# Attention with a gated feed-forward: other positions for the outer query products, both score tiles first from block 16 on, weight sums later on GpSimd, and the x addition on GpSimd

## The chip, the core and the metric

One Trainium2 chip, and of it one core. A core has five engines that run their own instruction streams and meet at semaphores: TensorE (PE, matrix products; its weight loads are shown apart as PEld), VectorE (DVE), ScalarE (ACT), GpSimd (POOL) and SyncE (SP), which here issues all the DMAs after the start. PE writes its products to PSUM, eight banks of 128 x 512 floats. The metric is the time of one execution in microseconds; lower is better.

## What is computed

x is 2048 x 512 in bf16. There are 32 heads of width 128, with keys and values of 2048 positions from a cache. The result is

```
xn = layernorm(x)
q  = xn @ wq                                  # per head, 2048 x 128
p  = softmax(q @ k_cache.T * 128**-0.5)
s  = concat(p @ v_cache) @ wo                 # 2048 x 512
gate, up = xn @ W_gate, xn @ W_up             # 2048 x 1792
g  = silu((relu(gate) * up) @ W_down)
out = x + s * g
```

## The kernel before

**Blocks and positions.** The attention is cut into 128 blocks: head h by head, and in each head four query tiles Q of 512 rows. A block has 8 positions. At a position PE multiplies two key tiles of 128 with the query tile (the score pair: two products of 128 x 512, line 1467), ACT takes the exponential of both at once (line 1479), and PE multiplies a pair of such exponentials with the values (8 products of 128 x 129, line 1576, called PV below). PV runs three positions behind the scores, so at each step of the main loop (line 1767) PE gets the score pair of position gp = gq + 3 and the PV of position gq. A block and a position named below are those of gq. When a block's last PV is done, DVE normalizes it (reciprocal and Onorm, lines 1496 and 1499); the first PV of the next block waits for that, since both use the same two PSUM banks.

**The ring.** The other six banks make three slots of two banks (`ring_acquire`, line 389). A score pair takes a slot and gives it back when its exponential is done. Other products on PE, called items, take slots from the same ring and give them back when DVE has read the result. Slots are handed out in turn. A slot that is held (`hold=True`) leaves the ring until `ring_release`, which puts it second in line; meanwhile the score pairs alternate between the two that are left.

**The items.** All the projections that the attention needs are put between score pairs and PV by a plan that is written out by hand (`plan`, filled by `at(block, position, item)`, lines 1642 to 1748); `side` does the same for work that gives PE nothing. The projections use Strassen's seven products. Blocks 0 to 15 carry the rest of the gated feed-forward (`emit_gu`, `emit_d`), the query projections of the first heads (`emit_st`) and sums of weights on POOL (`gu_sums`, `emit_sw`). From block 16 on there are two kinds of items:
- `emit_os`, at position 0 of a block: one step of the output projection of the four heads of the last group of 16 blocks, four steps for four blocks. Steps 0, 1 and 2 give PE 8 products of 128 x 256 and DVE two or three additions; step 3 gives PE 4 products. The blocks of step 3 (those that leave 3 when divided by 4) are called early: there PE issues the score pairs of positions 0 and 1 before the item, and none at position 1.
- `emit_unit`: the query projections of the group of heads after next, as seven units of seven products, 42 units in all: in each stretch of 16 blocks seven, starting in blocks that are two apart, from block 21 to block 113 (`unit_at`, line 941). A unit has six steps. Step 0 takes and holds a slot and issues two products, steps 1, 2 and 3 one each into the same banks, and step 3 releases the slot; in the next block step 4 takes and holds a slot again, and step 5 releases it. Between the steps DVE reads the sums out (line 1038), and a step waits for DVE's reading of the step before. POOL prepares the operands of a unit beforehand (`prep_unit`), and after two of the seven units it adds four sums (`add_unit`, line 1104) on which the next unit's DVE work waits.

**Positions of the unit steps** (line 1720): in the first block 2, 3, 5, 6, in an early block 3, 4, 6, 7; in the second block 3, 5, or 5, 7 if the block after it is early. An item at position 7 is issued ahead of the score pair (`ahead_of_S`).

**Order of scores and PV.** At a position with an item, or while a unit holds a slot, or at position 7 ahead of an early block, PE gets both score tiles and then both PV tiles. At every other position the two are interleaved (`split`, line 1818): score tile, PV tile, score tile, PV tile.

**POOL and DVE beside it.** `emit_wx` (line 1293) scales and sums output weights on POOL, once for 16 blocks; `emit_ox` (line 1308) forms four sums of attention outputs on DVE, twice for 16 blocks. In blocks 117 to 127 `emit_base` (line 1439) makes the part of the output that is known by then, s_acc times g plus x, with two DVE operations for each of 16 tiles.

## Time and profile before

| | us |
|---|---|
| median of 3 runs (lowest, highest) | 1259.94 (1259.73, 1260.38) |
| the profiled execution | 1260.08 |
| its span, first to last instruction | 1258.7 |
| of it outside the span | 1.4 |
| granted TensorE clock | 1.00 throughout |

The rows of the profile itself are shown where they are used. How they are read: a row of the timeline has the start, the duration from the first start to the last end of a merged run, the engine (a q behind it marks the sequencer), the line of the kernel, the operation, what is written and read, its shape, and how many instructions were merged; brackets give the idle time of that engine before it and what ended it. A row of the waits has who waited for whom, the total in us, how often, and the longest. A row of the stretches has, for each engine, busy time and number of instructions. PE's products are pipelined: one of 128 x 512 is shown with 0.38 us, but the next one starts 0.22 us later, so the room that a product takes is read from the starts. A weight load runs beside the products, and its wait is no loss as long as it is over when the product before it is. Some product records are missing from the trace (12130 beside 12353 weight loads); there the starts are further apart without any wait.

### The profile page before, as it was taken

The numbers are of one execution on the slowest core, as the hardware profiler recorded it, in microseconds if no ns is written. First come the engines' busy times: TensorE is split into PE (matmuls) and PEld (weight loads), VectorE is DVE, ScalarE is ACT, GpSimd is POOL, SyncE is SP. The second block draws the span as 40 slices with busy tenths as digits, with TensorE's granted clock in tenths as the row PEclk, the third lists the DMA queues.
The fourth block names the chain that finished last, engine by engine and source line by source line (L and its number), as shares of the span: only waits on it lengthen the run. The fifth ranks groups of instructions, "written<-read, shape, count | busy, mean of one in ns | idle before, by whom it ended". The sixth has DMA issues, their size and how long they took to land.

```text
span 1258.7 us, 29145 instructions
## 1 busy us (share of the span) xinstructions
PE 1237.9 (98%) x12130; PEld 860.1 (68%) x12353; DVE 809.6 (64%) x1328; ACT 1031.1 (82%) x1109; POOL 597.0 (47%) x606
## 2 busy tenths in 40 slices
PE   9999999999999999999999999999999999999998
PEld 5466666776677676667766676667676676767775
DVE  7677877665565747564665647564766547674487
ACT  4457877667888898888888898889888898889994
POOL 3473876415634377343855357534835456530002
PEclk9999999999999999999999999999999999999999
DMA  9712331324122332323222232233222222235222
GB/s 272 155 31 43 72 77 23 54 43 117 40 43 47 77 60 47 52 64 68 51 31 41 66 61 52 47 68 68 48 51 50 43 58 47 51 64 144 59 52 76
DMA packets 254914, 82.25 MB, mean 65 GB/s; under 512 B 226368, under 2 KB 254784, under 8 KB 254784
## 3 DMA queue, kind: packets, MB, share of 16 engines
q1 hardware_dynamic: 254112, 79.98, 30.7%
q8 instruction: 98, 1.61, 0.6%
q10 hardware_dynamic: 672, 0.39, 0.1%
q14 instruction: 32, 0.26, 0.1%
HBM read 40.63 MB, written 4.19 MB: 36 GB/s over the span
## 4 chain that ended last, share of the span: by engine, by line
PE 80%; ACT 9%; issue 8%; DVE 2%; POOL 0%; DMA 0%; DVEq 0%; POOLq 0%
PE ps_acc L1576 30%; PE ps_r L1467 27%; ACT PT L1479 9%; PE ps_r L1348 5%; PE ps_r L1033 5%; PE ps_r L1145 3%; PE ps_r L1206 3%; PE ps_r L711 2%; PE ps_r L715 2%; PE ps_r L896 2%; PE ps_acc L814 1%; DVE UVR L1038 1%; DVE QT_sb L1038 1%; POOL g_sb L1631 0%; DVE OX L1322 0%
## 5 line engine op out<-in xcount | busy, mean ns | idle before, releaser
L1479 ACT ACTIVATE PT<-ps_r 128x1024 bf16<-128x1024 f32 x1024 | 979.8, 1032 | 158.4 <-PE ps_r L1467 151.5
L1576 PEld LDWEIGHTS ps_acc<-V_sb,PT 128*128 128x128 bf16 x8192 | 582.7, 98 | 211.0 <-ACT PT L1479 3.4
L1576 PE MATMUL ps_acc<-V_sb,PT 128*128 128x129 bf16 x8192 | 705.3, 220 | 7.2 <-DVE Onorm L1499 0.3
L1467 PE MATMUL ps_r<-QT_sb,KT_sb 128*128 128x512 bf16 x1835 | 619.1, 380 | 5.8 <-DVE QT_sb L1038 0.9
L1038 DVE TENSOR_TENSOR UVR<-UVR,ps_r 128x512 f32<-128x512 f32 (+1 forms) x228 | 165.7, 755 | 134.1 <-PE ps_r L1033 130.2
L1467 PEld LDWEIGHTS ps_r<-QT_sb,KT_sb 128*128 128x128 bf16 x2048 | 173.2, 98 | 19.4 <-DVE QT_sb L1038 7.3
L1366 DVE TENSOR_TENSOR s_acc<-s_acc,ps_r 128x512 f32<-128x512 f32 x264 | 167.6, 683 | 11.4 <-PE ps_r L1348 10.5
L1496 DVE RECIPROCAL rz_sb<-ps_acc 128x4 f32<-128x4 f32 x127 | 22.9, 181 | 133.6 <-PE ps_acc L1576 132.8
L1005 POOL TENSOR_TENSOR TI<-xn_sb 128x512 f16<-128x512 f16 x48 | 57.7, 1202 | 88.4 <-PE ps_r L1033 88.4
L1038 DVE TENSOR_TENSOR QT_sb<-UVR,ps_r 128x512 bf16<-128x512 f32 x72 | 49.1, 687 | 65.2 <-PE ps_r L1033 62.8
L1499 DVE TENSOR_TENSOR Onorm<-ps_acc,rz_sb 128x512 bf16<-128x512 f32 x127 | 87.8, 691 | 4.4
L979 POOL TENSOR_SCALAR Wq_sb<-Wq_sb 128x1024 bf16<-128x1024 bf16 x12 | 33.2, 2768 | 117.5 <-DMA Wq_sb<-in_A_wq_dram 117.5
L1005 POOL TENSOR_TENSOR TI<-xnT 128x512 f16<-128x512 bf16 x36 | 41.6, 1155 | 71.0 <-PE ps_r L1033 70.2
L1631 POOL TENSOR_TENSOR g_sb<-s_acc,WX 128x512 bf16<-128x512 f32 x6 | 6.8, 1154 | 124.2 <-DVE WX L1624 124.2
L1104 POOL TENSOR_TENSOR QT_sb<-UVR,UVR 128x512 bf16<-128x512 f32 x24 | 32.1, 1367 | 62.3 <-DVE UVR L1038 62.3
L1104 POOL TENSOR_TENSOR UVR<-UVR,UVR 128x512 f32<-128x512 f32 x24 | 29.7, 1269 | 61.5 <-DVE UVR L1038 61.5
L1005 POOL TENSOR_TENSOR TI<-xn_sb,TI 128x512 f16<-128x512 f16 x48 | 55.5, 1156 | 0.0
L1033 PE MATMUL ps_r<-TI,SI 128*128 128x512 f16 x126 | 48.2, 382 | 2.2 <-DVE UVR L1038 2.2
L1348 PE MATMUL ps_r<-WX,OX 128*128 128x256 f16 x336 | 45.8, 273 | 0.0
L1005 POOL TENSOR_TENSOR TI<-xnT,TI 128x512 f16<-128x512 bf16 x36 | 41.6, 1156 | 0.0
L1121 POOL TENSOR_SCALAR gB<-gB 128x512 bf16<-128x512 bf16 x14 | 20.8, 1487 | 42.6 <-DVE gB L1151 42.6
L1348 PEld LDWEIGHTS ps_r<-WX,OX 128*128 128x128 f16 x336 | 32.9, 98 | 9.8 <-ACT PT L1479 1.8
(186 smaller groups left out, 1205.0 us busy)
## 6 DMA issues: line engine op xcount, KB each, us to landing
V_sb<-in_A_v_cache_dram SPq DMA_DIRECT2D x32, 512.0 KB, 4.4
Wq_sb<-in_A_wq_dram SPq DMA_DIRECT2D x16, 256.0 KB, 3.1
Wo_sb<-in_A_wo_dram SPq DMA_DIRECT2D x8, 512.0 KB, 4.7
out_dram<-g_sb SPq DMA_DIRECT2D x4, 512.0 KB, 4.7
g_sb<-out_dram SPq DMA_DIRECT2D x4, 512.0 KB, 6.6
xr_sb<-in_A_x_dram SPq DMA_DIRECT2D x16, 128.0 KB, 2.0
OT_store<-Onorm SPq DMA_TRANSPOSE x127, 2.5
Wd_sb<-in_B_W_down_dram SPq DMA_DIRECT2D x1, 1792.0 KB, 14.5
```

Of the source, the lines that this page charges most:

```text
L1005: return sem_ui.sig(pool.tensor_tensor(dst, x, y, o))
L1033: return sem_up.sig(pe.matmul(dst, lhs, rhs, start=start, stop=stop, skip_group_check=True))
L1038: dve.tensor_tensor(dst, x, ps, ALU.add))
L1104: u_tok["add"] = sem_uv.sig(pool.tensor_tensor(dst, UU[:, i, :], RR[:, i, :], ALU.add))
L1145: ins = pe.matmul(ps_r[:, bank, :], L(i), R(i), start=(i == 0), stop=(i == HC - 1))
L1206: ins = pe.matmul(ps_r[:, bank, j * DH:(j + 1) * DH], L(i), R(i), start=(i == 0 and j == 0), stop=(i == HF - 1 and j == 1))
L1348: ins = pe.matmul(ps_r[:, bank, j * DH:(j + 1) * DH], L(i), R(i), start=(i == 0 and j == 0), stop=(i == GH - 1 and j == 1))
L1366: t = dve.tensor_tensor(names[k], names[k], view(bank), op)
L1467: ins = pe.matmul(ps_r[:, 2 * s + tt, :], KT_sb[h % 2][:, t * 128:(t + 1) * 128], QT_sb[qt_slot[(h, Q)]][:], start=True, stop=True)
L1479: act.activation(PT[pb][:], ps_r[:, 2 * s:2 * s + 2, :], ACTF.Exp, scale=scale / WSC)
L1499: dve.tensor_tensor(Onorm[ob][:], o_ap, rz_sb[:].to_broadcast([128, 4, Dh]), ALU.mult))
L1576: ins = pe.matmul(o_ap, PT[pb][:, tt, j * 128:(j + 1) * 128], V_sb[vb][:, t, 0:VW], start=(t == 0 and j % 2 == 0), stop=(t == KT - 1 and j ...
```

## The change

- The steps of every unit move: to positions 1, 3, 5, 6 in the first block, early or not; in the second to 2, 4, or to 3, 6 if the block after it is early. Nothing is left at position 7, so `ahead_of_S` goes.
- Score and PV tiles are interleaved only below block 16 and only where there is no item. From block 16 on PE always gets both score tiles first.
- `emit_wx` of the groups in the middle is issued two blocks later (position 6 of the tenth block of 16 rather than the eighth).
- `emit_base`: the multiplication stays on DVE, the addition of x goes to POOL, with a semaphore of its own.
- At the start: the scaling of weights on ACT stays where it was, as `gu_scale`; the sums of it on POOL, `gu_sums(0)`, `(1)` and `(2)`, move from the last feed-forward stage and from block 0 to (block, position) (0, 7), (1, 3) and (1, 5), the first behind a wait for the newest exponential, and `emit_sw(1)`, the weights of the second head pair, from ahead of the loop to (1, 1). One copy of a query product from PSUM goes from ACT to DVE.

```diff
@@ gu_sums
+        def gu_scale(k):
+            W = W2[k % NW]
+            _wait(act, gu_tok[(k, "w")])
+            wflat = W[:].rearrange("p c i e -> p (c i e)")
+            gu_tok[(k, "s")] = sem_w2s.sig(act.activation(wflat, wflat, ACTF.Copy, scale=GSC))
+
         def gu_sums(k):
             W, X = W2[k % NW], SG[k % NW]
-            _wait(act, gu_tok[(k, "w")])
-            wflat = W[:].rearrange("p c i e -> p (c i e)")
-            t = gu_tok[(k, "s")] = sem_w2s.sig(act.activation(wflat, wflat, ACTF.Copy, scale=GSC))
-            _wait(pool, t)
+            if (k, "s") not in gu_tok:
+                gu_scale(k)
+            _wait(pool, gu_tok[(k, "s")])
@@ emit_gate_up
                     if fc in (7, 9):
-                        gu_sums((fc - 7) // 2)
+                        gu_scale((fc - 7) // 2)
@@ emit_st, step 0
-                if pr == 0 and c == 1:
-                    _wait_all(act, [p1, st_tok["r"]])
-                    st_tok["u"] = sem_qpa.sig(act.copy(cu[:], ps_r[:, banks[0], :]))
-                else:
-                    _wait(dve, p1)
-                    st_tok["u"] = sem_qpe.sig(dve.tensor_copy(cu[:], ps_r[:, banks[0], :]))
+                _wait(dve, p1)
+                st_tok["u"] = sem_qpe.sig(dve.tensor_copy(cu[:], ps_r[:, banks[0], :]))
@@ emit_base
-            _wait(dve, t1)
-            _wait(dve, sem_xr[k % 4].cur())
-            base_done[n] = sem_fin.sig(
-                dve.tensor_tensor(s_acc[:, n, :], s_acc[:, n, :], xr_sb[:, k % 4, :], ALU.add))
+            _wait(pool, sem_xr[k % 4].cur())
+            _wait(pool, t1)
+            base_done[n] = sem_fb.sig(
+                pool.tensor_tensor(s_acc[:, n, :], s_acc[:, n, :], xr_sb[:, k % 4, :], ALU.add))
@@ the plan of the units
-            first = (3, 4, 6, 7) if b in early else (2, 3, 5, 6)
-            second = (5, 7) if b + 2 in early else (3, 5)
-            for step, (r, p) in enumerate([(0, p) for p in first] + [(1, p) for p in second]):
+            second = (3, 6) if b + 2 in early else (2, 4)
+            for step, (r, p) in enumerate([(0, p) for p in (1, 3, 5, 6)] + [(1, p) for p in second]):
                 at(b + r, p, (emit_unit, 0, n, step))
-            if first[3] == NP - 1:
-                ahead_of_S.add(b)
@@ the main loop
-        emit_sw(1)
...
-            if pq == NP - 1 and bq in ahead_of_S:
-                for it in items:
-                    emit_M(it)
-                items = None
+            split = not ahead and not items and bq < GB
             if not ahead:
                 open_S_pair(gp)
                 emit_S_tile(gp, 0)
+                if not split:
+                    emit_S_tile(gp, 1)
...
+            if (bq, pq) == (0, 7):
+                _wait(pool, sem_exp.cur())
+                gu_sums(0)
+            if (bq, pq) == (1, 1):
+                emit_sw(1)
+            if (bq, pq) == (1, 3):
+                gu_sums(1)
             if pq == 4 and bq == 0:
+                gu_scale(2)
+            if (bq, pq) == (1, 5):
                 gu_sums(2)
...
-            if pq == 6 and bq % GB == 7 and 1 < bq // GB < NG - 1:
+            if (bq % GB, pq) == (9, 6) and 1 < bq // GB < NG - 1:
                 emit_wx(bq // GB)
             if items:
-                if not ahead:
-                    emit_S_tile(gp, 1)
...
-            split = not items and not ahead
-            if split and (u_held or (pq == NP - 1 and bq + 1 in early)):
-                emit_S_tile(gp, 1)
-                split = False
             emit_PV_tile(gq, 0)
             if split:
                 emit_S_tile(gp, 1)
```

More of the change, by code (lines that the diff above doesn't have):

```diff
@@ L270, in bass_recurrent_scan__mha_block_cached__glu_gated_reglu__prompt_kernel @@
         sem_da = newsem()
-        sem_qpa = newsem()
         sem_rz = newsem()
@@ L275, in bass_recurrent_scan__mha_block_cached__glu_gated_reglu__prompt_kernel @@
         sem_fin = newsem()
+        sem_fb = newsem()
         sem_sq = newsem()
@@ L943, in bass_recurrent_scan__mha_block_cached__glu_gated_reglu__prompt_kernel @@
         u_prep = {}
-        ahead_of_S = set()
         u_done = {}
```

## The prediction

> **What bounds the kernel now.** I read the page first, then busy time by stretch, then the waits of PE's weight loads, then timelines of single blocks.
>
> ```profile
> PE 1237.9 (98%) x12130; PEld 860.1 (68%) x12353; DVE 809.6 (64%) x1328; ACT 1031.1 (82%) x1109; POOL 597.0 (47%) x606
> PE 80%; ACT 9%; issue 8%; DVE 2%; POOL 0%; DMA 0%; DVEq 0%; POOLq 0%
> 322.44:1148.39 825.95, 814.40 (x8406) 579.24 (x8559) 507.08 (x814) 726.57 (x761) 418.49 (x428) 1.00 0.28 54
> 1164.30:1172.25 7.95, 7.84 (x89) 5.95 (x89) 5.30 (x10) 7.43 (x9) 0.00 (x0) 1.00 0.19 49
> 1172.25:1180.20 7.95, 7.90 (x89) 5.95 (x89) 5.21 (x10) 7.43 (x9) 0.00 (x0) 1.00 0.51 85
> ```
>
> PE is the bound at a granted clock of 1.00. The change removes no product, so only PE's waits can go, and their size is the first number to find. PE's busy share hides them, because a product is shown longer than its room. The third row is the stretch from the first PV of block 21 to that of block 116, 95 blocks with all 42 units. The last two rows are blocks 118 and 119: no unit, one output step of 8 products, 7.95 us each.
>
> ```profile
> 599.13 0.59 PE L1467 MATMUL ps_r<-QT_sb,KT_sb 128*128 128x512 bf16 x2
> 599.56 1.04 PE L1348 MATMUL ps_r<-WX,OX 128*128 128x256 f16 x8
> 600.43 1.06 PE L1576 MATMUL ps_acc<-V_sb,PT 128*128 128x129 bf16 x12
> 601.33 0.38 PE L1467 MATMUL ps_r<-QT_sb,KT_sb 128*128 128x512 bf16 x1
> 602.20 0.38 PE L1033 MATMUL ps_r<-xnT,Wq_sb 128*128 128x512 bf16 x1
> 602.64 0.62 PE L1576 MATMUL ps_acc<-V_sb,PT 128*128 128x129 bf16 x8
> ```
>
> From the starts: a score pair takes 0.43, an output step of 8 products 0.87, two unit products 0.44 (602.20 to 602.64, one record merged elsewhere) and one 0.216 (between 0.43/2 and 0.44/2), a PV pair 0.45 (8 products, 0.62 less 0.17 for the last one's tail). A plain position is 0.88. The stretch without waits: 95 x 7.95 = 755.3, less 24 early blocks with half a step (24 x 0.43 = 10.4), plus 42 x 7 unit products (294 x 0.216 = 63.5): 808.3. It took 825.95. **PE waits 17.6 us there**, 2.1% of it.
>
> ```profile
> PEld ps_r L1033 <- DVE UVR L1038: 15.0, 30, 0.9
> PEld ps_r L1467 <- DVE QT_sb L1038: 7.3, 17, 0.5
> PEld ps_r L1467 <- DVE UVR L1038: 5.1, 13, 0.4
> PEld ps_r L1033 <- DVE UVR L1037: 4.8, 12, 0.5
> ```
>
> These are idle times of the weight loads, over the whole run; most of each is covered by the product in front of it, so they don't add up to the 17.6. They name the culprit: a unit product (L1033) or a score (L1467) that wants what DVE reads out of a unit's slot.
>
> **Part 1: unit steps and tile order.** Three kinds of wait, each from one block.
>
> (a) Block 49, its unit after an `add_unit`:
>
> ```profile
> 564.20 5.34 POOL L1104 TENSOR_TENSOR QT_sb<-UVR,UVR 128x512 bf16<-128x512 f32 x4 [10.68 <-DVE UVR L1038]
> 569.62 1.88 DVE L1038 TENSOR_TENSOR UVR<-UVR,ps_r 128x512 f32<-128x512 f32 x3 [1.82 <-PE ps_r L1033]
> 570.37 0.39 PE L1033 MATMUL ps_r<-TI,SI 128*128 128x512 f16 x1 [0.36 <-DVE UVR L1038]
> ```
>
> POOL's four sums end at 569.54, DVE starts on step 0 there, and step 1 on PE waits for DVE. The old step 5 comes at position 5 of block 48; at position 4 POOL starts one position, 0.9 to 1.1, earlier, while step 1 stays at position 3. Against it: DVE's last two sums of block 48 (next part) now meet POOL's, which costs POOL an estimated 0.5. I leave 0.2 of the wait in each of 6 such blocks (1.2); bounds 0 and 0.4.
>
> (b) Block 56, where a score waits for the slot that step 5 releases:
>
> ```profile
> 630.75 1.61 POOL L1304 TENSOR_TENSOR WX<-Wo_sb,WX 128x512 f16<-128x512 bf16 x1
> 631.27 1.64 DVE L1322 TENSOR_TENSOR OX<-OX,OT_store 128x1024 f16<-128x1024 f16 x1
> 633.57 0.39 PE L1467 MATMUL ps_r<-QT_sb,KT_sb 128*128 128x512 bf16 x1 [0.19 <-DVE QT_sb L1038]
> 562.55 0.68 DVE L1322 TENSOR_TENSOR OX<-OX,OT_store 128x1024 f16<-128x1024 f16 x1
> ```
>
> The sum L1322 takes 0.68 in block 48 and 1.64 here, where it cannot start before POOL's L1304 is over (630.75 + 1.61 = 632.36, then 0.55 more). The change issues POOL's WX work at position 6 of block 57, after the sums, and step 5, one position earlier, has two of the four sums ahead of it on DVE instead of three. By starts from T, the first PV of block 56: step 4's product at T + 1.76 (0.45 + 0.88 + 0.43), DVE on it to 2.9, two sums of 0.6 to 4.1, step 5's product at 3.74, DVE on it to 4.87; the score that wants the slot comes at 5.28. No wait is left.
>
> The Trainium skill, page "SBUF — State Buffer", section "Who interferes with whom", states that a VectorE instruction with two SBUF inputs and a GpSimd instruction that reads SBUF exclude each other for a whole instruction, whichever starts first. By that rule L1322's extra 0.96 is the rest of L1304, which the trace bears out.
>
> (c) Two slots only. While a unit holds one, a score pair needs the exponential of the pair before last.
>
> ```profile
> 610.85 8.43 ACT L1479 ACTIVATE PT<-ps_r 128x1024 bf16<-128x1024 f32 x9 [0.70 <-PE ps_r L1467]
> 614.18 0.62 PE L1576 MATMUL ps_acc<-V_sb,PT 128*128 128x129 bf16 x8
> 614.68 0.60 PE L1467 MATMUL ps_r<-QT_sb,KT_sb 128*128 128x512 bf16 x2
> 598.33 2.90 ACT L1479 ACTIVATE PT<-ps_r 128x1024 bf16<-128x1024 f32 x3
> 601.75 3.00 ACT L1479 ACTIVATE PT<-ps_r 128x1024 bf16<-128x1024 f32 x3 [0.52 <-PE ps_r L1467]
> ```
>
> In block 54 the score is due at 614.18 + 0.45 = 614.63 and starts at 614.68: 0.05 late, because the pair before last was interleaved and its second tile came 0.23 (half a PV pair) later than need be. With both tiles first, from the second tile to the score that wants its slot PE has 0.45 + 0.43 + 0.45 = 1.33; ACT starts 0.2 after the second tile's room (601.33 + 0.22 to 601.75), takes 1.03 (mean 1032 ns), and the slot is back 0.07 later (the fourth of the nine starts at 610.85 + 3 x 0.91 = 613.58 and ends at 614.61; the score follows at 614.68): 1.30. It fits, by 0.03, if ACT is not behind.
>
> Is it? ACT does one in about 0.91 (9 in 8.43, which has one short pause), PE a plain position in 0.88, so ACT falls back 0.03 at each of seven and is idle after each item (0.70, 0.52). The new step 0 at position 1 gets the slot of position 0's pair. In block 53 that exponential ends at 601.23 in the old order; with T = 600.43 step 0 would come at T + 0.88 = 601.31. Both tiles first takes 0.23 off it. In early blocks it is closer: step 0 comes 0.43 (pair of position 1) + 0.43 (item) + 0.45 (PV) = 1.31 after the second tile, which needs 1.30 plus ACT's lag. I put 0.06 on each of the 18 early unit blocks (1.1); bounds 0 and 0.2. All later steps, followed like (b) with DVE's three readings in 1.88, have their operand 0.6 us or more ahead of PE.
>
> Part 1: 17.6 - 1.2 - 1.1 = 15.3 off.
>
> **Part 2: the start.**
>
> ```profile
> 72.77 0.58 ACT L911 COPY cuv<-ps_r 128x512 f32<-128x512 f32 x1
> 73.45 0.69 DVE L901 TENSOR_TENSOR QT_sb<-cuv,ps_r 128x512 bf16<-128x512 f32 x1 [1.34 <-ACT cuv L911]
> 73.60 0.39 PE L1576 MATMUL ps_acc<-V_sb,PT 128*128 128x129 bf16 x4
> 74.28 0.59 PE L1467 MATMUL ps_r<-QT_sb,KT_sb 128*128 128x512 bf16 x2 [0.29 <-DVE QT_sb L901]
> 78.57 2.77 POOL L641 TENSOR_SCALAR Wq_sb<-Wq_sb 128x1024 bf16<-128x1024 bf16 x1
> 74.25 1.12 POOL L618 TENSOR_TENSOR SG<-W 128x256 f16<-128x256 bf16 x1
> 90.00:96.00 6.00, 5.95 (x63) 4.93 (x63) 3.23 (x5) 3.88 (x5) 0.00 (x0) 1.00 0.01 3
> 96.00:102.00 6.00, 5.95 (x56) 4.15 (x55) 3.19 (x7) 4.99 (x7) 0.00 (x0) 1.00 0.00 0
> ```
>
> The score at 74.28 was due at 73.60 + 0.23 = 73.83. DVE's sum had waited 1.34 for ACT's copy, queued behind an exponential. On DVE the copy (0.69, like L901) runs in that gap, and the sum ends near 73.8: 0.45 off, bounds 0 and 0.45. The moved POOL work is at most 2.77 + 16 sums x 1.12 = 20.7, from about 86 on; POOL is empty from 90 to 102, and what comes first in line is needed first (first sums and scaled weights by block 2 at 102, the last by block 3, 114). I cost it at nothing; without that cover the gated products of block 2 would wait for POOL, up to 5 us.
>
> **Part 3: x on POOL.**
>
> ```profile
> 1202.97 0.69 DVE L1449 TENSOR_TENSOR s_acc<-s_acc,xr_sb 128x512 f32<-128x512 f32 x1
> 1203.58 0.17 DVE L1496 RECIPROCAL rz_sb<-ps_acc 128x4 f32<-128x4 f32 x1
> 1204.62 1.06 PE L1576 MATMUL ps_acc<-V_sb,PT 128*128 128x129 bf16 x12 [0.31 <-DVE Onorm L1499]
> L1104 POOL TENSOR_TENSOR UVR<-UVR,UVR 128x512 f32<-128x512 f32 x24 | 29.7, 1269 | 61.5 <-DVE UVR L1038 61.5
> ```
>
> 16 additions leave DVE (0.69) for POOL, nearest row 1.27. POOL has nothing else in blocks 117 to 127. Only once did they lie in PE's way: the addition at 1202.97 held the reciprocal back, and PE lost 0.3 or a little more. I take 0.3 off; bounds +0.3 (POOL's additions hold DVE's own two-input sums, as in (b)) and -0.5. SP waits for each addition 0.6 longer before it fetches the next x tile, which is fetched four tiles ahead.
>
> **Sum.** The profiled execution took 1260.08, 1.38 outside its span of 1258.7, 0.14 above the median. 1260.08 - 15.3 - 0.45 - 0.3 = 1244.0.
>
> **Rivals.**
> - *Longer holds.* A first hold now lasts from 1 to 6 instead of 2 to 6 or 3 to 7, a second one before an early block from 3 to 6 instead of 5 to 7: some 11 more plain positions with two slots in 16 blocks, 65 in all. At the 0.05 of (c) they cost 3, at twice that 6.5: 1247 to 1251. For it: a margin of 0.03. Against it: the 0.05 comes from the interleaved order.
> - *Slower: step 0 waits for ACT.* If ACT is one exponential (0.91) behind at position 0, step 0 waits 0.9 in 18 early blocks and some 0.5 in the 24 others: 28 more, 1272. It passes the old time once the mean wait is over 16/42 = 0.4. For it: in block 53's old order 0.08 was left. Against it: ACT is idle 0.5 to 0.7 after every item.
> - *POOL and DVE exclude each other* in new places (units' operands against the sums of block 56, x against DVE in the last blocks): (b) gives back 0.4 in 5 blocks, part 3 its 0.6: 1246.6.
> - *Nothing comes of it*: the waits for DVE only move to the next product, 1260. Against it: DVE is busy 507 of 826 us, and gets 0.9 more time before each use.
>
> **Chances.** Forecast, 1241 to 1247.5: 0.60. Longer holds, to 1252: 0.22. Exclusion is inside these, 0.04. Nothing: 0.03. Slower: 0.11. The range 1239.5 to 1254 leaves out 2 in 10 at most; its lower end is all 17.6 and the upper bounds of parts 2 and 3 with 2 us to spare. Within 0.2% (2.5 us, what a measurement can tell) counts as the same: faster 0.86, same 0.03, slower 0.11.
>
> **What would show it.** Right: blocks 21 to 115 take 809 to 812 us; block 56's sums take about 0.7 and no score waits for QT_sb there; block 49's step 1 waits 0.2 or less; the L1033 waits for UVR shrink to a fraction; the ACT copy is gone and the score after it starts 0.23 after the PV before. Wrong: score or unit products idle for ACT at positions 1 to 6 (longer holds, or the slower rival if it is at position 1), or POOL additions stretch DVE's rows after 1156.

## The result, and the profile after

| | us |
|---|---|
| before, median of 4 runs (lowest, highest) | 1260.12 (1259.73, 1260.38) |
| after, median of 4 runs (lowest, highest) | 1242.77 (1242.67, 1242.88) |
| after over before, with its 95% interval | 0.9863 (0.9846 to 0.988) |
| forecast (range) | 1244.0 (1239.5 to 1254) |
| span of the profiled execution, before and after | 1258.7, 1241.5 |

The kernel is 17.35 us faster, and 1.2 us below the forecast time. First the page of the kernel after: the busy times, and the chain of work that ended last.

```profile
PE 1223.8 (99%) x12125; PEld 863.6 (70%) x12353; DVE 804.2 (65%) x1313; ACT 1035.3 (83%) x1108; POOL 615.1 (50%) x622
PE 96%; issue 2%; POOL 1%; ACT 0%; DMA 0%; DVE 0%; SPq 0%; POOLq 0%; DVEq 0%
```

The work is the same (12353 weight loads), but the chain now runs through PE for 96% of the span instead of 80%: hardly any product on that chain waits for another engine. Next, busy time by stretch of the kernel after, from the first PV of block 21 to that of block 116 (length, then busy time of PE, PEld, DVE, ACT and POOL with their counts, granted clock, DMA share, GB/s), and its waits of PE's weight loads (total, times, longest).

```profile
321.87:1131.61 809.74, 801.15 (x8400) 583.11 (x8559) 510.31 (x814) 731.18 (x761) 418.02 (x428) 1.00 0.29 55
```

```profile
PEld ps_r L1348 <- ACT PT L1479: 7.0, 24, 0.3
PEld ps_r L1033 <- DVE s_acc L1366: 4.7, 18, 0.3
PEld ps_acc L1576 <- ACT PT L1479: 2.6, 10, 0.3
PEld ps_r L1033 <- DVE UVR L1038: 2.6, 6, 0.4
```

The stretch took 825.95 and takes 809.74: 16.2 of the 17.35. Its products need 808.3. Of the 72 weight loads that waited for what DVE reads out of a unit's slot (30 + 17 + 13 + 12) six are left, 0.4 each, and no score waits for such a reading. The other three rows are loads that wait while the product before them still runs; the block lengths below show that they cost nothing or nearly so.

**Block 56.** The timeline of DVE, of POOL and of PE's scores in the kernel after; the block's first PV is at 620.49.

```profile
623.35 0.68 DVE L1317 TENSOR_TENSOR OX<-OT_store 128x1024 f16<-128x1024 bf16 x1
623.95 0.68 DVE L1319 TENSOR_TENSOR OX<-OT_store 128x1024 f16<-128x1024 bf16 x1
624.73 0.69 DVE L1038 TENSOR_TENSOR QT_sb<-UVR,ps_r 128x512 bf16<-128x512 f32 x1
625.34 1.07 DVE L1322 TENSOR_TENSOR OX<-OX,OT_store 128x1024 f16<-128x1024 f16 x1
624.71 1.15 POOL L1005 TENSOR_TENSOR TI<-xn_sb 128x512 f16<-128x512 f16 x1 [9.20 <-PE ps_r L1033]
625.80 0.59 PE L1467 MATMUL ps_r<-QT_sb,KT_sb 128*128 128x512 bf16 x2
```

The two sums ahead of step 5's reading take 0.68 each, the reading ends at 625.42, and the score of position 6 starts at 625.80, which is T + 5.31 where the prediction had 5.28. L1322 behind the reading still takes 1.07: POOL's L1005 runs until 625.86, and L1322 ends 0.55 later. Nobody waits for it.

**Block 49.** POOL, DVE and PE around step 1 in the kernel after.

```profile
558.00 5.80 POOL L1104 TENSOR_TENSOR QT_sb<-UVR,UVR 128x512 bf16<-128x512 f32 x4 [9.93 <-DVE UVR L1038]
563.89 3.14 DVE L1038 TENSOR_TENSOR UVR<-UVR,ps_r 128x512 f32<-128x512 f32 x4 [1.40 <-PE ps_r L1033]
564.63 0.10 PEld L1033 LDWEIGHTS ps_r<-TI,SI 128*128 128x128 f16 x1 [0.43 <-DVE UVR L1038]
```

POOL's four sums are still what DVE waits for, and they became longer (5.34 to 5.80). They also start 0.9 earlier against the first PV of block 49 (561.36 here, 566.68 before) and so end 0.42 earlier. The idle time of step 1's weight load is still 0.43, most of it under the product before it: by the block lengths below the product is late by 0.12 instead of 0.54.

**The start and the end.** The kernel after, block 0, then DVE and POOL in block 122.

```profile
72.36 0.69 DVE L915 COPY cuv<-ps_r 128x512 f32<-128x512 f32 x1 [0.18 <-PE ps_r L901]
73.15 0.69 DVE L906 TENSOR_TENSOR QT_sb<-cuv,ps_r 128x512 bf16<-128x512 f32 x1
73.68 0.39 PE L1576 MATMUL ps_acc<-V_sb,PT 128*128 128x129 bf16 x4
73.91 0.60 PE L1467 MATMUL ps_r<-QT_sb,KT_sb 128*128 128x512 bf16 x2
```

```profile
1184.97 2.58 POOL L1449 TENSOR_TENSOR s_acc<-s_acc,xr_sb 128x512 f32<-128x512 f32 x2 [32.48 <-DVE s_acc L1444]
1186.27 0.18 DVE L1496 RECIPROCAL rz_sb<-ps_acc 128x4 f32<-128x4 f32 x1 [0.84 <-PE ps_acc L1576]
```

The score follows its PV by 0.23, as foreseen. In block 122 the reciprocal now waits for PE, not PE for the reciprocal: DVE is idle 0.84 ahead of it.

### The profile page after: what moved, and what is told of

It reads as the page before. It is cut to its first block, busy times and chain, and to the rows that moved or that the text cites. A ratio compares the mean times of both kernels' runs of the same rounds, so it can differ in the third digit from the quotient of the medians.

```text
span 1241.5 us, 29139 instructions
## 1 busy us (share of the span) xinstructions
PE 1223.8 (99%) x12125; PEld 863.6 (70%) x12353; DVE 804.2 (65%) x1313; ACT 1035.3 (83%) x1108; POOL 615.1 (50%) x622
## 4 chain that ended last, share of the span: by engine, by line
PE 96%; issue 2%; POOL 1%; ACT 0%; DMA 0%; DVE 0%; SPq 0%; POOLq 0%; DVEq 0%
PE ps_acc L1576 37%; PE ps_r L1467 34%; PE ps_r L1348 7%; PE ps_r L1033 5%; PE ps_r L1145 3%; PE ps_r L1206 3%; PE ps_r L901 2%; PE ps_r L720 2%; PE ps_r L716 2%; PE ps_acc L819 1%; POOL g_sb L1631 1%; ACT PT L1479 0%; DMA x_sb<-in_A_x_dram 0%; PE ps_r L1611 0%; PE ps_r L528 0%
## 5 line engine op out<-in xcount | busy, mean ns | idle before, releaser
L1576 PEld LDWEIGHTS ps_acc<-V_sb,PT 128*128 128x128 bf16 x8192 | 550.0, 98 | 213.3 <-ACT PT L1479 2.6
L1576 PE MATMUL ps_acc<-V_sb,PT 128*128 128x129 bf16 x8192 | 638.7, 220 | 2.0
L1467 PE MATMUL ps_r<-QT_sb,KT_sb 128*128 128x512 bf16 x1836 | 564.8, 379 | 8.8
L1038 DVE TENSOR_TENSOR UVR<-UVR,ps_r 128x512 f32<-128x512 f32 (+1 forms) x228 | 168.3, 755 | 107.2 <-PE ps_r L1033 104.3
L1467 PEld LDWEIGHTS ps_r<-QT_sb,KT_sb 128*128 128x128 bf16 x2048 | 160.6, 98 | 7.3 <-ACT PT L1479 0.3
L1005 POOL TENSOR_TENSOR TI<-xn_sb 128x512 f16<-128x512 f16 x48 | 58.2, 1212 | 126.3 <-PE ps_r L1033 126.3
L1449 POOL TENSOR_TENSOR s_acc<-s_acc,xr_sb 128x512 f32<-128x512 f32 x16 | 20.6, 1308 | 98.9 <-DVE s_acc L1444 65.0
L1104 POOL TENSOR_TENSOR QT_sb<-UVR,UVR 128x512 bf16<-128x512 f32 x24 | 34.8, 1479 | 59.6 <-DVE UVR L1038 59.6
L1005 POOL TENSOR_TENSOR TI<-xn_sb,TI 128x512 f16<-128x512 f16 x48 | 55.6, 1159 | 0.0
L1005 POOL TENSOR_TENSOR TI<-xnT 128x512 f16<-128x512 bf16 x36 | 41.6, 1154 | 23.6 <-PE ps_r L1033 22.8
L1005 POOL TENSOR_TENSOR TI<-xnT,TI 128x512 f16<-128x512 bf16 x36 | 41.7, 1158 | 0.0
L1290 POOL TENSOR_SCALAR Wo_sb<-Wo_sb 128x2048 bf16<-128x2048 bf16 x7 | 37.5, 5363 | 0.6
```

The source lines that it names most:

```text
L1005: return sem_ui.sig(pool.tensor_tensor(dst, x, y, o))
L1038: dve.tensor_tensor(dst, x, ps, ALU.add))
L1104: u_tok["add"] = sem_uv.sig(pool.tensor_tensor(dst, UU[:, i, :], RR[:, i, :], ALU.add))
L1290: k = sem_wx.sig(pool.tensor_scalar(wflat, wflat, WOSC, None, op0=ALU.mult))
L1467: ins = pe.matmul(ps_r[:, 2 * s + tt, :], KT_sb[h % 2][:, t * 128:(t + 1) * 128], QT_sb[qt_slot[(h, Q)]][:], start=True, stop=True)
L1576: ins = pe.matmul(o_ap, PT[pb][:, tt, j * 128:(j + 1) * 128], V_sb[vb][:, t, 0:VW], start=(t == 0 and j % 2 == 0), stop=(t == KT - 1 and j ...
```

## The experiments

All medians are in one table; the kernel before had 1260.11 to 1260.24 beside them. The other columns are lengths of blocks, from the start of a block's first PV weight load to that of the next block's. "Room" is 7.95 for a block with an output step of 8 products (7.52 with step 3's four), plus 0.216 for each unit product, so what is above it is PE waiting. Each ratio has an interval of up to 0.0017 to either side, 2 us, so that some of these kernels can't be told from the kernel after by their medians alone. What carries the small differences is the block lengths of the profiled executions: a block near which nothing was changed has the same length to within 0.03 from kernel to kernel, block 0 apart.

| kernel | median us | 48 | 49 | 53 | 54 | 55 | 56 |
|---|---|---|---|---|---|---|---|
| room | | 8.38 | 9.03 | 9.03 | 8.38 | 8.60 | 8.38 |
| before | 1260.12 | 8.51 | 9.57 | 9.11 | 8.62 | 8.73 | 8.88 |
| weight sums moved only | 1258.18 | 8.51 | 9.57 | 9.11 | 8.62 | 8.73 | 8.51 |
| tile order only | 1256.72 | 8.41 | 9.57 | 9.11 | 8.53 | 8.73 | 8.88 |
| unit steps only | 1253.15 | 8.39 | 9.15 | 9.03 | 8.48 | 8.62 | 9.78 |
| after, weight sums back | 1249.71 | 8.39 | 9.14 | 9.03 | 8.39 | 8.62 | 9.78 |
| after, interleaved back | 1245.08 | 8.38 | 9.15 | 9.03 | 8.48 | 8.62 | 8.38 |
| after, second block back | 1246.29 | 8.38 | 9.57 | 9.03 | 8.38 | 8.62 | 8.39 |
| after, step 0 back | 1245.51 | 8.39 | 9.15 | 9.11 | 8.38 | 8.70 | 8.39 |
| after | 1242.77 | 8.38 | 9.15 | 9.04 | 8.38 | 8.62 | 8.38 |
| after, OX sums earlier | 1242.36 | 8.38 | 9.03 | 9.03 | 8.39 | 8.63 | 8.38 |
| after, OX sums earlier but not in 16 | 1242.06 | 8.38 | 9.03 | 9.03 | 8.38 | 8.63 | 8.38 |
| after, ACT late by one copy | 1244.37 | 8.38 | 9.14 | 9.03 | 8.39 | 8.71 | 8.38 |
| after, ACT late by five | 1253.33 | 8.38 | 9.13 | 9.24 | 8.38 | 9.10 | 8.38 |

The same lengths, added up over blocks 21 to 115, say where PE waited, in us above the room:

| blocks | before | tile order only | unit steps only | after |
|---|---|---|---|---|
| 6 like 49 (unit behind POOL's sums) | 3.3 | 3.3 | 0.7 | 0.7 |
| 5 like 56 (weight sums beside step 5) | 2.5 | 2.5 | 7.0 | 0.0 |
| 24 like 54 (second block, ahead of an early one) | 6.5 | 4.4 | 2.4 | 0.1 |
| 18 like 55 (early, first block) | 2.0 | 2.0 | 0.4 | 0.4 |
| the other 42 | 3.3 | 2.0 | 0.1 | 0.1 |
| all | 17.5 | 14.1 | 10.6 | 1.3 |

The largest part lies in the 24 blocks like 54. The late tile makes 2.1 of their 6.5. Most of the rest is a wait for DVE: with step 5 at position 7, the second score pair that the early block issues ahead of its item wants the slot that step 5 releases, and in each of the 24 its weight load was idle 0.39 or 0.46 for DVE's reading (they are 24 of the 17 + 13 waits of L1467 in the kernel before). With the unit steps alone none of these is left.

**Unit steps only**, on the kernel before:

```diff
-            first = (3, 4, 6, 7) if b in early else (2, 3, 5, 6)
-            second = (5, 7) if b + 2 in early else (3, 5)
+            first = (1, 3, 5, 6)
+            second = (3, 6) if b + 2 in early else (2, 4)
```

> The kernel before with the new positions of the unit steps and nothing else. Theory of the prediction: the 15.3 of part 1 come only with all three edits. The waits (a) and the many small DVE waits go, but the weight sums on POOL still run in the blocks like 56, where step 5 now stands behind two of the four OX sums that are locked out by them: the score of position 6 starts near T + 6.85 instead of T + 5.28, 1.57 in each of 5 blocks (7.9), and the waits (c), 0.07 for each of 42 holds, stay (3). 1260.1 - 15.3 + 7.9 + 3 = 1255.7, bounds 1253 to 1258. Rival, the place of the weight sums is indifferent: 1248. Rival, the tile order does it all: 1260, and the blocks 49 and 53 wait as before.

Measured 1253.15, ratio 0.9946 (0.9931 to 0.9961). It lies just inside the lower bound given: block 56 got worse by 0.9 (8.88 to 9.78; 1.4 above its room, 1.57 expected), and only the 24 second blocks like 54 kept a wait of kind (c), 0.10 each, 2.4 in all and not 3. Both rivals fall.

**Weight sums back**, on the kernel after:

```diff
-            if (bq % GB, pq) == (9, 6) and 1 < bq // GB < NG - 1:
+            if pq == 6 and bq % GB == 7 and 1 < bq // GB < NG - 1:
                 emit_wx(bq // GB)
```

> The changed kernel with the weight sums on POOL put back to position 6 of the eighth block of 16. Theory: in the blocks 40, 56, 72, 88 and 104 the OX sums on DVE again take 1.6 instead of 0.7 behind POOL's WX work, step 5 is read late and the score of position 6 waits 1.57: 1242.8 + 7.9 = 1250.7, bounds 1248 to 1252, all of it in these five blocks. Rival, the move does nothing once the steps stand elsewhere: 1242.8.

Measured 1249.71, ratio 0.9917 (0.9903 to 0.9932): 6.9 slower than the kernel after, all of it in the five blocks named (5 x 1.40 = 7.0). The waits of PE's weight loads in this kernel, and its timeline in block 56:

```profile
PEld ps_r L1467 <- DVE QT_sb L1038: 7.0, 5, 1.4
```

```profile
624.41 1.15 POOL L1304 TENSOR_TENSOR WX<-Wo_sb,WX 128x512 f16<-128x512 bf16 x1
625.64 1.48 POOL L1306 TENSOR_TENSOR WX<-WX,Wo_sb 128x512 f16<-128x512 f16 x1
624.49 1.62 DVE L1317 TENSOR_TENSOR OX<-OT_store 128x1024 f16<-128x1024 bf16 x1
626.04 1.64 DVE L1319 TENSOR_TENSOR OX<-OT_store 128x1024 f16<-128x1024 bf16 x1
627.60 0.68 DVE L1038 TENSOR_TENSOR QT_sb<-UVR,ps_r 128x512 bf16<-128x512 f32 x1
628.33 0.61 PE L1467 MATMUL ps_r<-QT_sb,KT_sb 128*128 128x512 bf16 x2 [1.23 <-DVE QT_sb L1038]
```

Read it by ends: POOL's L1304 ends at 625.56, and the first sum, begun at 624.49, ends 0.55 later. L1306, begun at 625.64, ends at 627.12, and the second sum 0.56 later. Each sum waits out POOL's instruction and then does its own work, and the reading of step 5 stands behind both. The reading itself, with one operand in PSUM, takes 0.68. The page "SBUF — State Buffer" of the Trainium skill, section "Who interferes with whom", says that the second to start is blocked until the first is through; these rows agree.

**Weight sums moved only**, on the kernel before: the same line, the other way round.

> The kernel before with the weight sums on POOL two blocks later and nothing else. Theory: in the blocks 40, 56, 72, 88 and 104 the OX sums shrink to 0.7, and their 0.51 falls to the 0.14 of blocks 44 and 60, which have the same old steps without weight sums: 5 x 0.37 = 1.9 off, 1258.3, bounds 1257.5 to 1259. That is a quarter of what the same move is worth behind the new steps (6.9). Rival, it is worth the same in both places: 1253.3. Rival, nothing: 1260.2.

Measured 1258.18, ratio 0.9984 (0.9975 to 0.9993), 1.9 faster, block 56 at 8.51 like 48. So the same move is worth 1.9 behind the old steps and 6.9 behind the new ones.

**Tile order only**, on the kernel before:

```diff
-            if split and (u_held or (pq == NP - 1 and bq + 1 in early)):
+            if split and (bq >= GB or pq == NP - 1 and bq + 1 in early):
```

> The kernel before with both score tiles first from block 16 on and nothing else. Theory: only the waits of kind (c) go, scores that start 0.02 to 0.10 late for their slot with no DVE wait behind them, some 0.7 in 16 blocks: 4 us, 1256, bounds 1254.5 to 1258; blocks 49 and 56 keep their 0.55 and 0.51. Rival, the late second tile is the cause of nearly all waits: 1244 to 1246. Rival, the order of tiles is indifferent: 1260.

Measured 1256.72, ratio 0.9973 (0.9963 to 0.9983): 3.4 faster. Blocks 49, 53, 55 and 56 don't move at all; the 24 like 54 and 13 like 48 get shorter by 0.09 to 0.10 each.

**Interleaved back**, on the kernel after:

```diff
-            split = not ahead and not items and bq < GB
...
+            split = not items and not ahead
+            if split and (u_held or (pq == NP - 1 and bq + 1 in early)):
+                emit_S_tile(gp, 1)
+                split = False
             emit_PV_tile(gq, 0)
```

> The changed kernel with score and PV tiles interleaved again from block 16 on wherever there is neither an item nor a held slot (the rule of the kernel before). Theory: where a hold begins behind an interleaved pair, the score after it is 0.05 to 0.10 late, once for each of 42 holds in the second blocks, little in the first blocks, where the pair ahead of the hold has an item: 1242.8 + 2 to 4, 1245 to 1247. Rival of the longer holds: interleaving leaves no margin anywhere, 6 or more, 1249 and up. Rival, the order is indifferent: 1242.8.

Measured 1245.08, ratio 0.988 (0.9864 to 0.9897): 2.3 slower than after, 0.10 in each of the 24 second blocks in which step 4 stands at position 3 behind an interleaved pair (54: 8.38 to 8.48), nothing in first blocks. Block 54, first in the kernel after, then here:

```profile
608.12 0.62 PE L1576 MATMUL ps_acc<-V_sb,PT 128*128 128x129 bf16 x8
608.57 0.59 PE L1467 MATMUL ps_r<-QT_sb,KT_sb 128*128 128x512 bf16 x2
```

```profile
607.92 0.62 PE L1576 MATMUL ps_acc<-V_sb,PT 128*128 128x129 bf16 x8
608.48 0.59 PE L1467 MATMUL ps_r<-QT_sb,KT_sb 128*128 128x512 bf16 x2
```

The score of position 5, two positions behind step 4, starts 0.45 after its PV pair in the kernel after, which is on time, and 0.56 after it with interleaved tiles. That is the low end of the theory's size, and only a part of its place: the 18 other second blocks, like 48 and 56, where step 4 at position 2 also stands behind an interleaved pair, lose nothing. No run shows why.

**Second block back**, on the kernel after, and **step 0 back**, on the kernel after:

```diff
-            second = (3, 6) if b + 2 in early else (2, 4)
+            second = (3, 6) if b + 2 in early else (3, 5)
```

> The changed kernel with steps 4 and 5 at positions 3 and 5 instead of 2 and 4 in the 18 second blocks that have no early block behind them. Theory: the slot of step 5 is back too late for the score two positions on (0.12 in each, 2.2), and in the 6 blocks like 48 POOL's four sums start a position later, so that step 1 of the block after waits 0.42 more, as before (2.5): 1242.8 + 4.7 = 1247.5, bounds 1246 to 1248.5. Rival, the wait of block 49 went for another reason: 1245 at most, and block 49 stays at 0.13. Rival, nothing: 1242.8.

Measured 1246.29, ratio 0.9888 (0.9874 to 0.9903): 3.5 slower. Half of the expectation held: block 49 is back at 9.57. Its timeline:

```profile
559.59 5.34 POOL L1104 TENSOR_TENSOR QT_sb<-UVR,UVR 128x512 bf16<-128x512 f32 x4 [10.80 <-DVE UVR L1038]
565.02 3.14 DVE L1038 TENSOR_TENSOR UVR<-UVR,ps_r 128x512 f32<-128x512 f32 x4 [1.82 <-issue]
565.77 0.39 PE L1033 MATMUL ps_r<-TI,SI 128*128 128x512 f16 x1 [0.36 <-DVE UVR L1038]
```

POOL starts when step 5 has been read, and its end sets DVE and step 1. The six blocks behind the other `add_unit`, like 45 and 61, lost 0.14 to 0.15 each, which I had not listed. The score two positions behind step 5, however, is on time everywhere (48 and 56 at their room): of the 0.13 that block 48 had before, the tile order alone takes 0.10 (8.51 to 8.41), so this position without interleaved tiles costs nothing there. 6 x 0.42 + 6 x 0.145 = 3.4.

```diff
-            for step, (r, p) in enumerate([(0, p) for p in (1, 3, 5, 6)] + [(1, p) for p in second]):
+            for step, (r, p) in enumerate([(0, p) for p in (2, 3, 5, 6)] + [(1, p) for p in second]):
```

> The changed kernel with step 0 of every unit at position 2 instead of 1 (steps 1, 2, 3 stay at 3, 5, 6). Theory: step 1 comes one plain position behind step 0, and DVE's first reading of step 0 is over too late for its weight load, 0.065 in each of 36 units as in the block 53 of before (2.3), while the 0.03 of the 18 early blocks goes (0.5): 1242.8 + 1.8 = 1244.6, bounds 1243.8 to 1245.5; block 49 keeps its 0.13, since POOL sets it. Rival, the first block's steps carry most of the gain: 1250 or more. Rival, nothing: 1242.8.

Measured 1245.51, ratio 0.9882 (0.9865 to 0.9898): 2.7 slower, 0.07 to 0.08 in each of 36 units (0.14 in block 21), and block 49 as foreseen unmoved. The early blocks lost as much as the others (8.62 to 8.70), where I had let them win back 0.03. The waits of the weight loads in this kernel have a row that the kernel after doesn't have:

```profile
PEld ps_r L1033 <- ACT PT L1479: 6.3, 18, 0.3
```

These are the 18 early blocks. Step 0 at position 2 takes the slot of the next score pair, whose exponential comes right behind that of the pair before, since an early block issues both pairs ahead of its item. So step 0 still has no margin against ACT: in block 55 it starts at 614.38, 0.02 after its room, and step 1 is late for DVE besides.

**Copy and x back**, on the kernel after, two parts 1100 us apart:

```diff
-                _wait(dve, p1)
-                st_tok["u"] = sem_qpe.sig(dve.tensor_copy(cu[:], ps_r[:, banks[0], :]))
+                if pr == 0 and c == 1:
+                    _wait_all(act, [p1, st_tok["r"]])
+                    st_tok["u"] = sem_qpa.sig(act.copy(cu[:], ps_r[:, banks[0], :]))
+                else:
+                    _wait(dve, p1)
+                    st_tok["u"] = sem_qpe.sig(dve.tensor_copy(cu[:], ps_r[:, banks[0], :]))
...
-                pool.tensor_tensor(s_acc[:, n, :], s_acc[:, n, :], xr_sb[:, k % 4, :], ALU.add))
+                dve.tensor_tensor(s_acc[:, n, :], s_acc[:, n, :], xr_sb[:, k % 4, :], ALU.add))
```

> The changed kernel with two parts undone that lie 1100 us apart: the query copy of block 0 on ACT again, and the addition of x on DVE again. Theory: block 0 gets its wait back, 0.45 to 0.63, and block 122 its 0.3 to 0.5 (the addition ahead of the reciprocal), everything else is unchanged: 1242.8 + 0.95 = 1243.7, bounds 1243.4 to 1244.0. Rival for block 0, the moved POOL work and not the copy made its gain: block 0 stays without a wait. Rival for the end, POOL's additions cost DVE as much as they save: nothing changes after block 116.

Measured 1243.65, ratio 0.9869 (0.9854 to 0.9884): 0.88 slower. From the starts of its PV products, block 0 takes 15.59 (before 15.78, after 15.14), so the copy is worth 0.45. The rest, 0.43, is the x addition: block 122 has 8.57 again (before 8.56, after 8.04), of which 0.06 comes back in block 123; no other block from 1 to 126 differs by more than 0.025. By the blocks the two parts make 0.93, by the medians 0.88.

**ACT late.** The kernel after with n small copies ahead of one exponential for each unit, n = 1 and 5. They only write a tile that nobody reads.

```diff
+        slow_at = {NP * b for _, _, b in unit_at}
...
             _wait(act, stok)
             pb = gp % NPB
+            if gp - LAG in slow_at:
+                for i in range(n):
+                    act.copy(idle_sb[:, 6 * i:6 * i + 6], ident[:, 0:6])
```

> The changed kernel with one small ACT copy ahead of the exponential of the score pair that is issued at position 0, in the first block of each of the 42 units; it delays that exponential by d. Tests the slower rival: step 0 at position 1 takes that pair's slot. By its mechanism the 18 early blocks have no margin (they lose d each), the 24 others have 0.45 (0.87 of the output step): loss = 18 d + 24 max(0, d - 0.45). d estimated at 0.14 from the two shapes of ACT rows (0.58 for 512 columns, 1.03 for 1024): 1242.8 + 2.5 = 1245.3. Rival, the slot is back well ahead everywhere and the forecast was never at risk: 1242.8. Rival, ACT falls behind for good: 6 or more.

> The same with five small copies, d estimated at 0.7. By the slower rival's mechanism: 18 x 0.7 + 24 x 0.25 = 18.6, so 1261.4, back at the time of the kernel before; the early blocks lose d, the others d - 0.45, and later positions nothing more. Rival, margin everywhere: under 5. Rival, the delay is handed on from pair to pair: over 30.

Measured 1244.37, ratio 0.9875 (0.9859 to 0.9891), and 1253.33, ratio 0.9945 (0.9931 to 0.996): 1.6 and 10.6 slower than after. Both are below my numbers because the copies delay less than I took. The kernel with five, early block 55 and the waits of weight loads:

```profile
614.76 0.57 ACT L1482 COPY idle_sb<-ident 128x6 bf16<-128x6 bf16 x5
615.23 1.93 ACT L1484 ACTIVATE PT<-ps_r 128x1024 bf16<-128x1024 f32 x2
616.30 0.10 PEld L1034 LDWEIGHTS ps_r<-xnT,Wq_sb 128*128 128x128 bf16 x1 [0.47 <-ACT PT L1484]
```

```profile
PEld ps_r L1034 <- ACT PT L1484: 18.8, 42, 0.5
```

From 614.76 to 615.23 five copies delay the exponential by 0.47, 0.095 each. Step 0 (L1034 here) is as much later: block 55 is longer by 0.48 with five and by 0.09 with one. The 24 others lost nothing with one copy and 0.09 in the mean with five: 0.20 in five like 53, about 0.09 in 13 like 61, nothing in the six like 49. With the measured delays the formula gives 18 x 0.095 = 1.7 and 18 x 0.475 + 24 x 0.025 = 9.2; what is missing to 10.6 is the margin of the others, 0.45 by my formula and by their losses 0.27 in the five like 53 and 0.39 in the 13. In the early blocks the mechanism of the slower rival is real, one for one; and the delay is not handed on (blocks 54 and 56 keep their 8.38).

**OX sums earlier**, on the kernel after:

```diff
-    side.setdefault((b0 + 7 * c, 1 + i) if c and g == NG - 2 else (b0 + 8 * c, 2 + i), []).append((emit_ox, g, c, i))
+    side.setdefault((b0 + 7 * c, 1 + i) if c and g == NG - 2 else (b0 + 8 * c, 1 + i + c), []).append((emit_ox, g, c, i))
```

> The changed kernel with the four OX sums of the blocks 32, 48, 64, 80, 96 and 112 one position earlier (1 to 4 instead of 2 to 5), so that POOL's four unit sums of these blocks meet fewer of them. Theory: POOL's sums end earlier, DVE reads step 0 of the next block earlier, and the 0.11 that is left in each of the blocks 33, 49, 65, 81, 97 and 113 goes: 1242.8 - 0.6 = 1242.2, bounds 1242.0 to 1242.8. Rival, POOL's start and not its length sets that wait: 1242.8. Rival, the sums now push step 5's reading back and the wait grows: 1243.5.

Measured 1242.36, ratio to before 0.986 (0.9845 to 0.9874). The step against the kernel after, 0.4, is small beside these intervals; the trace carries it: block 49 is at its room, 9.03, and so are the five others. POOL and DVE in block 48, first of the kernel after, then of this one:

```profile
558.00 1.66 POOL L1104 TENSOR_TENSOR QT_sb<-UVR,UVR 128x512 bf16<-128x512 f32 x1 [9.93 <-DVE UVR L1038]
559.61 1.73 POOL L1104 TENSOR_TENSOR QT_sb<-UVR,UVR 128x512 bf16<-128x512 f32 x1
558.55 1.65 DVE L1325 TENSOR_TENSOR OX<-OT_store,OX 128x1024 f16<-128x1024 bf16 x1
```

```profile
558.02 5.35 POOL L1104 TENSOR_TENSOR QT_sb<-UVR,UVR 128x512 bf16<-128x512 f32 x4 [9.93 <-DVE UVR L1038]
557.86 0.68 DVE L1325 TENSOR_TENSOR OX<-OT_store,OX 128x1024 f16<-128x1024 bf16 x1
563.46 1.28 DVE L1038 TENSOR_TENSOR UVR<-UVR,ps_r 128x512 f32<-128x512 f32 x2 [0.94 <-PE ps_r L1033]
```

In the kernel after the last OX sum waits for POOL's first sum (to 559.66) and POOL's second waits for the OX sum (to 560.20, then 1.14). With the sums a position earlier only POOL's first meets one, the last, which was there before it and keeps its 0.68; POOL's four take 5.35, and DVE starts on step 0 at 563.46 instead of 563.89. Six times 0.11 is 0.7, though, and 0.4 came: block 16, whose sums the edit also moves and where nothing was late before, became 0.32 longer. DVE and PE there, in this kernel:

```profile
277.27 1.64 DVE L1317 TENSOR_TENSOR OX<-OT_store 128x1024 f16<-128x1024 bf16 x1
278.83 0.68 DVE L1319 TENSOR_TENSOR OX<-OT_store 128x1024 f16<-128x1024 bf16 x1
279.43 0.68 DVE L1322 TENSOR_TENSOR OX<-OX,OT_store 128x1024 f16<-128x1024 f16 x1
280.03 1.27 DVE L1364 COPY s_acc<-ps_r 128x512 f32<-128x512 f32 x2
281.96 0.11 PEld L1467 LDWEIGHTS ps_r<-QT_sb,KT_sb 128*128 128x128 bf16 x2 [0.32 <-DVE s_acc L1366]
```

As in the kernel after, the first sum waits for the last weight sum that POOL does in block 16, but here three sums stand ahead of the readings of the output step, and the score that wants their slot is late: block 56 in small. Hence a last kernel, which leaves block 16 as it was:

```diff
-    side.setdefault((b0 + 7 * c, 1 + i) if c and g == NG - 2 else (b0 + 8 * c, 2 + i), []).append((emit_ox, g, c, i))
+    side.setdefault((b0 + 7 * c, 1 + i) if c and g == NG - 2 else (b0 + 8 * c, 2 + i - (c == 0 and g > 0)), []).append((emit_ox, g, c, i))
```

> As the last one, but the OX sums of block 16 stay at positions 2 to 5. With them one position earlier block 16 had become 0.32 longer (8.82 to 9.14), by the same lock: its first sum met the last of POOL's weight sums (1.63 instead of 0.68), and a score waited 0.32 for DVE's reading behind it. Theory: block 16 is back at 8.82 and the blocks 33, 49, 65, 81, 97 and 113 stay at 9.03: 1242.4 - 0.3 = 1242.05, bounds 1241.9 to 1242.3. Rival, the 0.32 of block 16 is not from the sums: 1242.4.

Measured 1242.06, ratio to before 0.9856 (0.984 to 0.9873): block 16 is back at 8.82, the six blocks stay at 9.03, and this kernel has the lowest median of all. The expectation has one thing wrong: the first sum did not become long by moving. It takes 1.64 in this kernel too, and in the kernel after. What had made block 16 late is the third sum ahead of the reading; here only two stand there, and that is in time:

```profile
277.56 1.64 DVE L1317 TENSOR_TENSOR OX<-OT_store 128x1024 f16<-128x1024 bf16 x1
279.12 0.68 DVE L1319 TENSOR_TENSOR OX<-OT_store 128x1024 f16<-128x1024 bf16 x1
279.72 1.28 DVE L1364 COPY s_acc<-ps_r 128x512 f32<-128x512 f32 x2
```

## Why the prediction was right, step by step

- **PE waits 17.6 in blocks 21 to 115** (825.95 against 808.3): it held (24 x 0.43 is 10.3 and not 10.4, which makes it 17.5, as the sum of the block lengths does). 16.2 of it went, 15.3 had been forecast; the stretch takes 809.74 where 809 to 812 was named. But the three blocks that the prediction worked out stand for only some 9 of the 17.5: 3.3 for (a), 2.5 for (b) and, by the run with the tile order alone, 3.4 for (c). In block 54, its example for (c), the late tile makes 0.09 of 0.24; the larger wait there, for DVE's reading of step 5 at position 7, it did not work out. That these other 8 us would go rested on one sentence, that all later steps have their operand 0.6 or more ahead of PE. The unit steps alone show that it was so: outside the blocks like 49 and 56 they leave 3.0 of 11.8, and the tile order takes 2.4 of that.
- **(a) 0.2 left in 6 blocks**: 0.12 is left (9.15 against 9.03), 0.5 us better in all. The estimate that POOL's sums lose 0.5 to DVE's was right (0.46, 5.34 to 5.80), and undoing the second block's positions brings back the 0.42 that the earlier start saves on balance. It also brings back 0.14 in the six blocks like 45, whose wait I had not told apart.
- **(b) no wait left in block 56**: right (8.88 to 8.38), and by the cause named: with the weight sums back the block is 1.40 longer. That all sums of the block would take 0.7 was wrong for the last two (1.07 and 0.80 in the kernel after), which meet the preparation of the next unit on POOL; the two that stand ahead of step 5 take 0.68.
- **(c) both tiles first, 0.06 left in 18 early blocks**: the order is worth 2.3 in the changed kernel, at the place named, the hold behind an interleaved pair. Interleaving makes a block 0.10 longer and not 0.05. Early blocks keep 0.02 to 0.03, not 0.06: another 0.5 us better.
- **Part 2, 0.45 from the copy**: 0.45 measured (15.59 to 15.14 in block 0). That the moved POOL work costs nothing was right about its cost and missed a gain of 0.19, also in block 0 (15.78 to 15.59). In the kernel before, DVE's L1228 took 1.15 beside POOL's SW sums, and the query behind it was late for a score; in the kernel after the same operation takes 0.68. The rows of the kernel before:

```profile
82.05 0.99 POOL L650 TENSOR_TENSOR SW<-Wq_sb 128x256 f16<-128x256 bf16 x1
82.43 1.15 DVE L1228 SCALAR_TENSOR_TENSOR g_sb<-dbuf,dbuf 128x512 bf16<-128x512 f32 x1
84.70 0.68 DVE L901 TENSOR_TENSOR QT_sb<-cuv,ps_r 128x512 bf16<-128x512 f32 x1
85.43 0.11 PEld L1467 LDWEIGHTS ps_r<-QT_sb,KT_sb 128*128 128x128 bf16 x2 [0.19 <-DVE QT_sb L901]
```

  This is read from the rows; no run moved that POOL work alone, so the cause of the 0.19 is argued and not shown. Some of it comes and goes by itself: in the kernel with the tile order alone, whose block 0 is that of the kernel before, the block took 15.69 and not 15.78.
- **Part 3, 0.3**: 0.43 measured, at the place named; the addition held the reciprocal longer than I had taken. POOL's addition takes 1.31 (1.27 estimated). DVE's multiplication beside it went from 0.68 to 0.80 in the mean, 16 x 0.12 = 1.9 us of DVE, for which nobody waits.
- **The sum**: 1244.0 was 1.2 too high. The four terms that were mis-sized make 0.5 (a) + 0.5 (c) + 0.19 + 0.13 = 1.3. All four erred to the same side, so the small error is not one of terms that cancelled.
- **The rivals.** Longer holds: they cost at most 0.5 (the 0.02 to 0.03 of the early blocks) and nothing elsewhere. Nor are they what makes interleaved tiles dear: those cost 2.3 beside the new holds and 3.4 beside the old, shorter ones. So the reason given against this rival, that the lateness comes from the interleaved order, was right. POOL against DVE: it shows in blocks 48 and 56 and at the end, and costs PE 0.7 in one kind of block, those like 49, which the last experiments take away. The slower rival didn't come to pass, but it was the right one to fear: the 18 early blocks have no margin at all. Five copies, 0.475 of delay, cost 10.6; from there a further delay costs the 36 units that already lose, so by these numbers the old time is reached at about 0.475 + (17.35 - 10.6) / 36 = 0.66, an estimate that takes the six like 49 to stay free.

What the prediction did not see is how much the three edits of part 1 depend on each other. Alone they bring 7.0 (steps), 3.4 (order) and 1.9 (weight sums), 12.3 together; in one kernel they bring 16.2, all of it in blocks 21 to 115, where the copy and the x addition change nothing. The steps alone put a reading behind two locked-out sums, a wait of 1.4 instead of 0.5 in five blocks, and the move of the weight sums, worth 1.9 by itself, is worth 6.9 there because it takes that away. The tile order goes the other way: 3.4 by itself, 2.3 beside the new steps, which already free the blocks like 48 (8.41 with the order alone, 8.39 with the steps alone). +5.0 and -1.1 make the 3.9 between 12.3 and 16.2.

## What to carry to other kernels

When one engine is 98% busy, its waits can hide in its busy share: add up the room of its products from the starts, compare with the length of the stretch, and place the difference block by block. When a step is moved, look at what stands ahead of its reading on the other engine and at who can lock that out there; a second edit worth little by itself may be what makes the first one pay. Before trusting a margin of hundredths, delay the operation in question by a known amount and see whether the loss follows one for one.

## What the runs showed of the hardware

- In these traces sums of DVE and POOL with both operands in SBUF take turns, both ways, and a record's length holds the time blocked: DVE's sum 1.65 instead of 0.68, POOL's 1.73 instead of 1.27. Where they meet once, the later row grows by a little less than the remainder of the other: 0.94 for 1.07 in block 56 with the weight sums back, 0.96 for 1.09 in block 56 of the kernel before, where the prediction put the two as equal.
- A DVE sum with one operand in PSUM is not held: in the kernel after, step 5's reading at 624.73 takes 0.69 beside POOL's L1005, which runs from 624.71 to 625.86, and the sum in SBUF behind it is held until L1005 ends.
- A small ACT copy (128 x 6) has a record of 0.21 in the mean, but five in a row put off the exponential behind them by 0.47, 0.095 each: here the price of an additional ACT instruction is read from the starts, not from the length of its record.
